# A fused attention, low-rank mixer and two MLPs on one core: new plan costs for the float32 products, earlier loads, other banks for the first scores, and products of ones in the plan's gaps

## The chip, the cores and the metric

The kernel runs on one core of a Trainium2 chip. The metric is the device time of one execution in microseconds (us); before the change it is 1762.4 us (median of 3 runs, 1760.25 to 1764.01). Engines are named as in the profile: PE (TensorE), DVE (VectorE), ACT (ScalarE), POOL (GpSimd) and SP (SyncE, which issues nearly all DMAs).

## The reference

An attention with mean-pooled keys and values, then a token mixer of rank 32 with an MLP, then a layer norm with a second MLP. Batch 8, 8 heads of 64, 576 positions, model width 512, MLP width 2048.

```
k_p, v_p = mean over groups of 8 positions of k, v          # 576 -> 72
scores   = q @ k_p.T / 8;  attn = exp(scores - max) / (sum + 1e-9)
x        = concat over heads of attn @ v_p                   # (8, 576, 512)

u = x + (x.T @ U @ V).T                                      # U 576x32, V 32x576
x = u + max(u @ w_ch1, 0) @ w_ch2                            # 512 -> 2048 -> 512

xn = (x - mean) / sqrt(var + 1e-6) * g_ln
out = x + max(xn @ w_ch1', 0) @ w_ch2'
```

U, V and the weights arrive as float64 words, which the kernel turns into float32 with five DVE or ACT operations on each tile of 512 words.

## The kernel before, in words

**The work.** A *pair* P is two heads of one batch; there are 32. Its steps on PE are five score products of 144 columns (`att_s`, L846), ten transposes of the exponentials (`att_t`, through `turn`, L399) and the products with the values. For the first eight pairs (`TM`) these are ten products of 65 columns (`tm_v`, L1028) and five products with U of 128 columns (`tm_g`, L1085), all in plain float32. Between them stand the row maximum (DVE, L871), the exponential (ACT, L880), copies out of PSUM (ACT or DVE, L404 and L406) and the division (DVE, L1049, L1056, L1066). The later pairs use float32r with the operand split into a high and a low part (L977, L978). The first MLP's first eight blocks of hidden channels run beside the attention, for groups of 512 tokens: `a_l1` (L1290, twelve products a block) and `a_l2` (L1318). The rest, three passes over nine groups of tokens, runs after it (L1519, L1607).

**The planner.** Each step is recorded by `Order.op` with the engines it may run on and what it costs there in ns. `schedule` plays all steps through on these costs and fixes the order of every engine's instructions. A step's priority is the PE time that was recorded before it (`clk`) plus a bias. The chip then runs each engine's list in that order, with semaphores where data or a buffer is awaited: a plan cost that is wrong changes an order, and no instruction's duration. The costs which the change touches are

```
att_s:  {PE: 4 * 2 * SP / 2.4}        # 240 ns a score product
tm_v:   {PE: 2 * len(tiles) * 200}    # 200 ns a product, 6 or 4 of them in a step
tm_g:   {PE: 5 * 240}                 # 240 ns a product, 5 in a step
cost *= SLOW if warm < 3000 else 1.0  # SLOW = 2.0: PE is planned at half rate until it was busy
```

**Buffers.** A buffer name is a ring of tiles: `q` 2, `k` 1, `v` 1, `xT` 5; the PSUM banks are `pa` 2 (sums of `a_l1`), `pbc` 2 (sums of `a_l2`) and `py` 4 (scores, transposes, value products). `att_load` issues k, q and v of a pair from SP; with one `k` tile the next pair's k waits until the last pair's was pooled (`att_prep`, L795, L798). `ones` is a constant 128x128 float32r tile that POOL fills at the start (L513).

Of the kernel before, what the change touches and what calls it, by code (L numbers as in the profile page):

```python
# [8 lines left out]
F32 = mybir.dt.float32  # L9
# [92 lines left out]

class Order:
    def __init__(self, nc, tc):
        self.nc, self.tc, self.ops, self.clk, self.bias = nc, tc, [], 0.0, 0.0

    def op(self, engs, fn, r=(), w=(), prio=None, size=0, full=False):
        o = Op()
        o.engs, o.fn, o.succs, o.size, o.full = engs, fn, [], size, full
        o.prio = (self.clk + self.bias) if prio is None else prio  # L110
        o.eng = o.end = o.start = None
        preds, bufs = set(), []
        for wr, lst in ((False, r), (True, w)):
            for x in lst:
                b, k = x if isinstance(x, tuple) else (x, None)
                if b not in bufs:
                    bufs.append(b)
                for k2, (lw, rd) in b.acc.items():
                    if k is None or k2 is None or k == k2:
                        if lw is not None:  # L120
                            preds.add(lw)
                        if wr:
                            preds.update(rd)
        for wr, lst in ((False, r), (True, w)):
            for x in lst:
                b, k = x if isinstance(x, tuple) else (x, None)
                if wr:
                    if k is None:
                        b.acc = {None: (o, [])}
                    else:  # L130
                        b.acc[k] = (o, [])
# [12 lines left out]
        o.ready = {e: 0.0 for e in engs}  # L144
        self.ops.append(o)
        if PE in engs:
            self.clk += engs[PE]
        return o


    def schedule(self):
# [6 lines left out]
        events, parked, order = [], {}, []  # L158
# [158 lines left out]
            at(e, free[e])  # L317
        self.total = max(o.end for o in self.ops)
        order.sort(key=lambda x: x[:2])
        return [o for _, _, o in order]  # L320

    def emit(self, pools, init):
        opened = set()
# [26 lines left out]
L_SAME = 100.0  # L350
L_PE = 320.0
L_ANY = 220.0
SLOW = 2.0
TURN = 98.0
CW = 2
KEEP = 50000.0
# [66 lines left out]
class Kern:  # L423
# [263 lines left out]
    def setup_v(self):  # L687
        nc, o = self.nc, self.o
        n = S // 4

        def load(raw):
            for c in range(4):
                o.op(
                    {SY: 450},
                    lambda e, c=c: e.dma_start(raw.t[c * RANK : (c + 1) * RANK, :n], self.V[:, c * n : c * n + n]),
                    w=[(raw, c)],
                    size=36864,
                )

        x = self.staged(n, load, "a")  # L700
        vh, vl = self.buf("vd"), self.buf("vd")
        o.op({ACT: c_act(n), DVE: c_fast(n)}, lambda e: copy(nc, e, vh.t, x.t[:, :n]), r=[x], w=[vh])
        o.op(
            {DVE: c_dve(n), GP: c_pool(n)},
            lambda e: e.tensor_sub(vl.t, x.t[:, :n], vh.t.bitcast(F32)),
            r=[x, vh],
            w=[vl],
        )
        for i, (y, copies) in enumerate(((vh, 3), (vl, 1))):
            d = Buf(None)  # L710
            for c in range(4):
                o.op(
                    {SY: 450},
                    lambda e, i=i, c=c, y=y: e.dma_start(
                        self.v_d[i, :, c * n : c * n + n], y.t[c * RANK : (c + 1) * RANK].bitcast(F32)
                    ),
                    r=[y],
                    w=[(d, c)],
                    size=18432,
                )  # L720
            for c in range(copies):
                r = (3 * i + c) * RANK
                o.op(
                    {SY: 450},
                    lambda e, i=i, r=r: e.dma_start(self.vst.t[r : r + RANK].bitcast(F32), self.v_d[i]),
                    r=[d],
                    w=[(self.vst, 3 * i + c)],
                    size=73728,
                )
# [43 lines left out]
    def att_load(self, P):  # L773
        o = self.o
        b, p = divmod(P, NP)
        q, k, v = self.buf("q"), self.buf("k"), self.buf("v")
        o.op({SY: 450}, lambda e: e.dma_start(k.t, self.kT[b, p]), w=[k], size=294912)
        o.op({SY: 450}, lambda e: e.dma_start(q.t, self.qT[b, p]), w=[q], size=294912)
        o.op(
            {SY: 450},  # L780
            lambda e: e.dma_start(v.t, self.v[b, 2 * p : 2 * p + 2].rearrange("h (k s) d -> k h (s d)", s=POOL)),
            w=[v],
            size=294912,
        )
        self.raw[P] = (q, k, v)

    def att_prep(self, P):
        nc, o = self.nc, self.o
        q, k, v = self.raw[P]
# [21 lines left out]

    def att_prep_v(self, P):
        o = self.o
        v = self.raw[P][2]
        vs = self.vs[P] = self.buf("v1" if P < TM else "vz" if P < LEAN_T else "vs")
        n = POOL * D
        while n > D:
            n //= 2
            to, w = (lambda n=n: v.t[:, :, :n]), [v]
# [4 lines left out]
            o.op(  # L824
                {GP: c_pool(2 * n), DVE: c_dve(2 * n)},
                lambda e, n=n, to=to: e.tensor_add(to(), v.t[:, :, :n], v.t[:, :, n : 2 * n]),
                w=w,
            )
        if P < LEAN_T:
# [1 line left out]
        self.split(  # L831
            View(vs, 0, lambda t: t[:, 0:4:3]),
            View(vs, 1, lambda t: t[:, 1:3]),
            View(v, None, lambda t: t[:, :, :D]),
            2 * D,
        )

    def att_s(self, P, t):
        q, kbd = self.qk[P]
        if t in (0, 3):  # L840
            self.sps[P, t // 3] = self.buf("py")
        ps = self.sps[P, t // 3]
        i = t % 3 * 2 * SP
        self.o.op(
            {PE: 4 * 2 * SP / 2.4},
            lambda e: e.matmul(  # L846
                ps.t[:, i : i + 2 * SP], q.t[:, QT[t] : QT[t] + 128], kbd.t.rearrange("p h n -> p (h n)"),
                start=True, stop=True, skip_group_check=True,
# [1 line left out]
            r=[q, kbd],  # L850
            w=[ps],
            full=True,
        )

    def att_m(self, P):
# [163 lines left out]
    def tm_v(self, P, z):  # L1019
# [11 lines left out]
                    )  # L1031

        r = [vs] + [(ef, j) for j in range(2 + z)]
        self.o.op({PE: 2 * len(tiles) * 200}, mm, r=r, w=[ps], full=True)

    def tm_n(self, P):
        o = self.o
# [36 lines left out]
    def tm_g(self, P):  # L1074
# [12 lines left out]
                )  # L1087

        r = [(x, (P, 0)), (x, (P, 1)), (x4, (P, 1)), self.us]
        self.o.op({PE: 5 * 240}, mm, r=r, w=[(pg, c)], full=True)  # L1090

    def tm_t(self, b, c):
        x, x4 = self.tx[b]
# [126 lines left out]
    def att_steps(self):  # L1220
# [6 lines left out]
        ld = lambda P: (lambda: self.att_load(P) if P < B * NP else None)  # L1227
        pr = lambda P: (lambda: self.att_prep(P))
        pv = lambda P: (lambda: self.att_prep_v(P))
        first = [ld(0), pr(0), pv(0), ld(1)] + [s(0, t) for t in range(5)] + [pr(1), pv(1), ld(2)]  # L1230
        first += [m(0)]
        for P in range(B * NP):
            N = P + 1
            last = P % NP == NP - 1
            S_ = [s(N, t) for t in range(5)] if N < B * NP else [None] * 5
            M_ = m(N) if N < B * NP else None
            R_ = [ld(P + 3), pr(P + 2), pv(P + 2)] if P + 2 < B * NP else [None] * 3
            T_ = [tt(P, j) for j in range(3)]
            V_ = [av(P, 0, 0), av(P, 1, 0), av(P, 0, 1), av(P, 1, 1)]
            if P < TM:  # L1240
                c = P % NP
                G = lambda c, P=P: [lambda: self.tm_g(P - P % NP + c)]
                W = [lambda P=P: self.tm_v(P, 0), lambda P=P: self.tm_v(P, 1), lambda P=P: self.tm_n(P)]
                seq = [S_[0], R_[2], S_[1], T_[0], S_[2], S_[3], T_[1], S_[4], T_[2], R_[1], M_]
# [6 lines left out]
                seq += [W[0], R_[0], W[1], W[2]]  # L1251
                if last:
                    b = P // NP
                    if b:
# [3 lines left out]
                    end = G(c) + [tt_[0], tt_[1], lambda b=b: self.att_gs(b), u[0], tt_[2], u[1], tt_[3], u[2], u[3], tt_[4], u[4]]  # L1258
                    seq += end
            elif not last:  # L1260
                seq = [S_[0], R_[2], S_[1], T_[0], S_[2], S_[3], T_[1], S_[4], T_[2], R_[1], M_, V_[0]]
                seq += [V_[1], R_[0], V_[2], V_[3]]
            else:
                b = P // NP
                x = [(lambda b=b, i=i: self.att_xt(b, i)) for i in range(5)]
                g = [(lambda b=b, i=i: self.att_g(b, i)) for i in range(5)]
                gs = lambda b=b: self.att_gs(b)
                vm = [(lambda b=b, h=h, c=c: self.att_vm(b, h, c)) for c in range(NCC) for h in range(2)]
                seq = [S_[0], R_[2], T_[0], S_[1], T_[1], S_[2], T_[2], V_[0], V_[1], S_[3], V_[2], V_[3], S_[4], R_[1]]
                seq += [M_, x[0], x[1], g[0], x[2], R_[0], g[1], x[3], g[2], x[4], g[3], g[4], gs]  # L1270
                seq += vm
            if P == 0:
                seq = first + seq
# [69 lines left out]
    def phase_a(self):  # L1343
# [2 lines left out]
        self.xT, self.xhl, self.ut, self.hid, self.wres = {}, {}, {}, {}, {}  # L1346
        self.ud, self.yd, self.wd = {}, {}, {}
        per = self.att_steps()
        self.lean = False
        for st in self.biased(per[0], E_BIAS):  # L1350
            st()
# [486 lines left out]
P_BIAS = -20000.0  # L1838
BACC = {"dynamic_dma_scratch_size": 2048}
TM = 2 * NP  # L1840
E_BIAS = -40000.0
LEAN_T = 8
LEAN_X = 8
W_LEAD = (-12000.0, 8000.0)
# [50 lines left out]
```

## Time and profile before

| | us |
|---|---|
| median of 3 runs | 1762.4 |
| the profiled execution | 1762.12 |
| its span, first to last instruction | 1760.3 |
| PE busy in the span | 1731.6 |
| PE busy in the first 140 us | 122.30 |
| DVE busy in the first 140 us | 117.32 |

The page gives the busy time of each engine; "idle before" in a row of the timeline is the time that the engine stood still ahead of that group of instructions and what ended it. In the trace a float32 product that isn't a transpose stands as two MATMUL records: the program's ten products of L1028 for a pair are a group of x20, its five score products x10. The granted clock is TensorE's, as a share of 2.4 GHz.

### The profile page before, as it was taken

What the parts mean: (1) busy time and instruction counts of PE and PEld (TensorE: products, weight loads), DVE (VectorE), ACT (ScalarE), POOL (GpSimd) and SP (SyncE); (2) the same over time, 40 slices, a digit from 0 to 9 for tenths busy, and PEclk for the clock granted to TensorE, in tenths of its full rate; (3) what the DMA queues carried; (4) which work ended last, traced back from release to release, by engine and by line L of the source; (5) the groups of instructions that cost most, each with busy time, mean ns of one, the idle gap of its engine ahead of it and who ended that gap; (6) DMA issues with size and microseconds to landing.
All of it is one profiled execution on the core that took longest, in us unless ns stands there. A gap on an engine that the chain in (4) does not pass through costs nothing.

```text
span 1760.3 us, 27152 instructions
## 1 busy us (share of the span) xinstructions
PE 1731.6 (98%) x10257; PEld 1526.3 (87%) x10257; DVE 975.9 (55%) x1834; ACT 732.0 (42%) x1843; POOL 790.9 (45%) x682
## 2 busy tenths in 40 slices
PE   7999999999999999999999999999999999999998
PEld 6788888888888889989999888999899999999897
DVE  6998887887745344444446866553224633333333
ACT  4665655655622224444444443333333432232221
POOL 3342222322100077777777863333335455555654
PEclk9999999999999999999999999999999999999999
DMA  6664654554243244444444344331112433333322
GB/s 191 197 193 161 208 173 139 192 182 131 98 147 121 79 166 120 121 120 120 120 120 113 128 129 154 131 128 66 48 49 85 144 102 102 105 120 105 102 78 78
DMA packets 96691, 222.99 MB, mean 127 GB/s; under 512 B 15408, under 2 KB 15792, under 8 KB 90800
## 3 DMA queue, kind: packets, MB, share of 16 engines
q1 hardware_dynamic: 96416, 221.26, 39.7%
q8 instruction: 80, 1.31, 0.3%
q14 instruction: 51, 0.42, 0.1%
q10 hardware_dynamic: 144, 0.00, 0.0%
HBM read 151.85 MB, written 69.37 MB: 126 GB/s over the span
## 4 chain that ended last, share of the span: by engine, by line
PE 87%; DVE 4%; DMA 2%; issue 0%; ACT 0%; DVEq 0%; SPq 0%; ACTq 0%
PE py L1607 33%; PE pa L1519 17%; PE pbc L1519 12%; PE pbc L1318 10%; PE pa L1290 9%; PE py L399 2%; PE py L846 1%; DMA wraw<-wC 1%; PE py L977 1%; PE py L978 1%; PE py L1184 0%; DMA w_d<-wx 0%; PE py L1015 0%; PE py L1014 0%; DMA xraw<-u_d 0%
## 5 line engine op out<-in xcount | busy, mean ns | idle before, releaser
L1607 PE MATMUL py<-hid,w2h 128*128 128x512 f32 x1728 | 541.3, 394 | 0.2 <-DVE hid L1547 0.2
L1607 PE MATMUL py<-hid,w2l 128*128 128x512 f32 x864 | 338.6, 392 | 0.0
L1519 PE MATMUL pa<-op,w1h 128*128 128x256 f32 x1728 | 326.1, 281 | 3.3 <-DVE pa L1583 3.0
L1519 PEld LDWEIGHTS pa<-op,w1h 128*128 128x128 f32 x1728 | 293.8, 188 | 40.2 <-DVE pa L1583 3.9
L1607 PEld LDWEIGHTS py<-hid,w2h 128*128 128x128 f32 x1728 | 273.6, 189 | 11.0 <-DVE hid L1547 0.5
L555 POOL TENSOR_TENSOR op<-xraw,op 128x512 fp32r<-128x512 f32 x130 | 171.3, 1321 | 247.5 <-ACT op L404 244.7
L1577 DVE TENSOR_TENSOR pbc<-s,pbc 128x512 f32<-128x512 f32 x108 | 75.1, 696 | 369.3 <-PE pbc L1519 369.1
L1519 PEld LDWEIGHTS pbc<-op,w1h 128*128 128x128 f32 x1296 | 220.6, 188 | 29.9 <-DVE s L406 1.8
L1519 PE MATMUL pbc<-op,w1h 128*128 128x256 f32 x1296 | 244.3, 281 | 1.4 <-DVE s L406 1.4
L1519 PE MATMUL pa<-op,w1l 128*128 128x256 f32 x864 | 242.6, 281 | 0.0
L1607 PEld LDWEIGHTS py<-hid,w2l 128*128 128x128 f32 x864 | 162.4, 188 | 36.7
L1318 PE MATMUL pbc<-op,wh 128*128 128x512 f32 x576 | 182.0, 397 | 0.0
L1519 PE MATMUL pbc<-op,w1l 128*128 128x256 f32 x648 | 181.8, 281 | 0.0
L1290 PE MATMUL pa<-hid,wh 128*128 128x512 f32 x576 | 180.4, 394 | 0.0
L1519 PEld LDWEIGHTS pa<-op,w1l 128*128 128x128 f32 x864 | 162.9, 189 | 0.0
L1547 DVE SCALAR_TENSOR_TENSOR hid<-pa,hid 128x512 fp32r<-128x512 f32 x108 | 74.5, 689 | 121.7 <-ACT hid L1541 121.6
L1541 ACT ACTIVATE hid<-pbc 128x512 fp32r<-128x512 f32 x108 | 64.7, 599 | 183.3 <-DVE pbc L1577 182.4
L1541 ACT ACTIVATE hid<-pa 128x512 fp32r<-128x512 f32 x108 | 64.6, 598 | 174.2 <-PE pa L1519 167.9
L1473 POOL TENSOR_TENSOR t<-xraw 128x512 f32<-128x512 f32 x52 | 67.8, 1305 | 131.8 <-DMA xraw<-n_d 73.0
L1290 PEld LDWEIGHTS pa<-hid,wh 128*128 128x128 f32 x576 | 105.8, 188 | 21.4 <-DVE op L1297 0.2
L1519 PEld LDWEIGHTS pbc<-op,w1l 128*128 128x128 f32 x648 | 121.9, 188 | 0.0
L1318 PEld LDWEIGHTS pbc<-op,wh 128*128 128x128 f32 x576 | 103.8, 188 | 19.4
(210 smaller groups left out, 2939.3 us busy)
## 6 DMA issues: line engine op xcount, KB each, us to landing
xraw<-n_d SPq DMA_DIRECT2D x18, 1024.0 KB
wraw<-wC SPq DMA_DIRECT2D x32, 512.0 KB
wraw<-wA SPq DMA_DIRECT2D x24, 512.0 KB
w_d<-wx SPq DMA_DIRECT2D x48, 256.0 KB
wraw<-w_d SPq DMA_DIRECT2D x48, 256.0 KB
k<-kT SPq DMA_DIRECT2D x32, 288.0 KB
q<-qT SPq DMA_DIRECT2D x32, 288.0 KB
v<-v SPq DMA_DIRECT2D x32, 288.0 KB
```

What stands on the lines that cost most here:

```text
L399: e.matmul(out, src, ident, start=first, stop=True, is_transpose=True, skip_group_check=True)
L555: lambda e: e.tensor_sub(lo(), src(), hi().bitcast(F32)),
L846: lambda e: e.matmul(ps.t[:, i : i + 2 * SP], q.t[:, QT[t] : QT[t] + 128], kbd.t.rearrange("p h n -> p (h n)"), start=True, stop=True, ski ...
L977: e.matmul(ps.t[:, :SH], w, eh.t[:, h, c], start=True, stop=False)
L1290: e.matmul(ps.t, w.t[:, c], u.t, start=(i == 0), stop=(i == 3 * NCC - 1))
L1318: e.matmul(ps.t, w.t[:, c], x.t, start=(f == 0 and j == 0), stop=(f == NA - 1 and j == 2))
L1473: o.op(on, lambda e: e.tensor_sub(dst(), a(), c()), r=r, w=w)
L1519: e.matmul(bank.t[:, sl], w.t[:, self.WCOL[k], c], u.t[:, t], start=(first and i == 0), stop=(last and i == 5), skip_group_check=True,)
L1541: lambda e: e.activation(h.t[:, :TG], bank.t, AF.Relu),
L1547: lambda e: e.scalar_tensor_tensor(l.t[:, :TG], bank.t, 0.0, h.t[:, :TG].bitcast(F32), op0=ALU.max, op1=ALU.subtract),
L1577: o.op({DVE: c_dve(TG)}, lambda e: e.tensor_add(c.t, s.t, c.t), r=[s], w=[c])
L1607: e.matmul(y.t, w.t[:, i, c], x.t[:, :TG], start=(first and q == 0), stop=(last and q == 2))
```

## The change

Seven edits, all of which act through the planner:

1. The PE costs of `att_s`, `tm_v` and `tm_g` become 123, 112 and 112 ns a product. Their old values stay as `lead`, what they add to the priorities' clock.
2. `SLOW` becomes 1.0: PE is planned at full rate throughout.
3. `filled` goes over the planned PE list. Where PE is planned idle between 1.3 and 140 us, it puts in as many products of `ones` with `ones` (512 columns, into a bank of `pa`, `pbc` or `py` that is planned free) as gaps of 225 ns fit. Their results are never read.
4. The k of pairs 1 and 3 goes to a tile of `xT` (`KX`), and v has a load step of its own (`att_load_v`), so that the first loads are issued as k, q, k, q, v.
5. Pooling of k of pair 1 is recorded ahead of v of pair 0.
6. The scores of the first four pairs (`EARLY`) go to `pa` instead of `py`.
7. `setup_v` loads V with one DMA instead of four, and writes each of its two parts with one instead of four.

```diff
-            self.clk += engs[PE]
+            self.clk += engs[PE] if lead is None else lead
...
+    def filled(self, order):
+        rings, fn = self.filler
...
+        extra, last = [], FILL[0]
+        for o in [o for o in order if o.eng == PE]:
+            if o.start > FILL[1]:
+                break
+            n = int((o.start - last) / FILL[2])
+            for k in range(n):
+                t = last + k * FILL[2]
+                best = None
+                for (r, i), spans in used.items():
+                    prev = max([e for s, e in spans if s <= t], default=-1e9)
+                    soon = min([s for s, e in spans if s > t], default=1e9)
+                    if prev + 500 <= t and soon >= o.start and (best is None or prev < best[0]):
+                        best = prev, r, i
+                if best is None:
+                    continue
+                z = Op()
+                z.eng, z.start, z.end, z.bufs = PE, t, t + FILL[2], ()
+                z.fn = lambda e, r=best[1], i=best[2]: fn(e, r.tiles[i])
+                extra.append(z)
+            last = o.end
...
-SLOW = 2.0
+SLOW = 1.0
...
-        q, k, v = self.buf("q"), self.buf("k"), self.buf("v")
+        q, k = self.buf("q"), self.buf("xT" if P in KX else "k")
...
-            self.sps[P, t // 3] = self.buf("py")
+            self.sps[P, t // 3] = self.buf("pa" if P < EARLY else "py")
...
-            {PE: 4 * 2 * SP / 2.4},
+            {PE: 123},
...
+            lead=4 * 2 * SP / 2.4,
...
-        self.o.op({PE: 2 * len(tiles) * 200}, mm, r=r, w=[ps], full=True)
+        self.o.op({PE: 2 * len(tiles) * 112}, mm, r=r, w=[ps], full=True, lead=2 * len(tiles) * 200)
...
-        self.o.op({PE: 5 * 240}, mm, r=r, w=[(pg, c)], full=True)
+        self.o.op({PE: 5 * 112}, mm, r=r, w=[(pg, c)], full=True, lead=5 * 240)
...
-        first = [ld(0), pr(0), pv(0), ld(1)] + [s(0, t) for t in range(5)] + [pr(1), pv(1), ld(2)]
+        first = [lk(0), lk(1), lv(0), pr(0), pr(1), lv(1), pv(0)] + [s(0, t) for t in range(5)] + [pv(1), lk(2), lv(2)]
...
+        self.o.filler = [self.R[a] for a in ("pa", "pbc", "py")], lambda e, ps: e.matmul(
+            ps, self.ones, self.ones.rearrange("p (o n) -> p o n", o=1).to_broadcast([128, 4, 128]),
+            start=True, stop=True, skip_group_check=True,
+        )
...
+KX = (1, 3)
...
+EARLY = 4
+FILL = (1300.0, 140000.0, 225.0)
```

All lines of the file move by about 40: L846, L1028, L1085, L399, L1290 and L1318 are L888, L1071, L1128, L439, L1334 and L1362 after it. The products of ones are L1393; the built program holds 155 of them, in 28 runs, and has the same other products on PE as before.

PE's list at the start of the program, from the scores of pair 0 to the value products of pair 0; before:

```order
L846 MATMUL py_253<-kbd_153,q_155 128x144 x3
L846 MATMUL py_254<-kbd_153,q_155 128x144 x2
L846 MATMUL py_255<-kbd_154,q_156 128x144 x2
L399 MATMUL py_256<-ident,sc_167 72x128 x4
L846 MATMUL py_255<-kbd_154,q_156 128x144
L846 MATMUL py_253<-kbd_154,q_156 128x144
L399 MATMUL py_254<-ident,sc_167 72x128 x4
L846 MATMUL py_253<-kbd_154,q_156 128x144
L399 MATMUL py_256<-ident,sc_167 72x64 x2
L1028 MATMUL py_254<-v_192,ef_166 128x65 x6
L1028 MATMUL py_256<-v_192,ef_166 128x65 x4
```

and now:

```order
L1393 MATMUL pa_249<-ones 128x512 x15
L888 MATMUL pa_249<-kbd_153,q_155 128x144 x3
L888 MATMUL pa_250<-kbd_153,q_155 128x144 x2
L1393 MATMUL pbc_251<-ones 128x512 x11
L888 MATMUL pa_249<-kbd_154,q_156 128x144 x3
L888 MATMUL pa_250<-kbd_154,q_156 128x144
L439 MATMUL py_253<-ident,sc_167 72x128 x4
L439 MATMUL py_254<-ident,sc_167 72x128 x4
L888 MATMUL pa_250<-kbd_154,q_156 128x144
L439 MATMUL py_255<-ident,sc_167 72x64 x2
L1393 MATMUL pbc_251<-ones 128x512 x3
L1071 MATMUL py_256<-v_192,ef_166 128x65 x6
```

29 products of ones stand among the first pair's work, 15 of them ahead of everything.

The same list at the value products of the pair of `vs_162` and the next scores, where the last of the products of ones stand; before, the MLP's products (L1318) stand there:

```order
L978 MATMUL py_253<-el_174,vs_162 128x288
L1318 MATMUL pbc_252<-op_200,wh_227 128x512
L1318 MATMUL pbc_252<-op_201,wh_227 128x512
L1318 MATMUL pbc_252<-op_200,wl_228 128x512
L1318 MATMUL pbc_252<-op_202,wh_229 128x512
L1318 MATMUL pbc_252<-op_203,wh_229 128x512
L1318 MATMUL pbc_252<-op_202,wl_230 128x512
L977 MATMUL py_255<-eh_173,vs_162 128x288
```

and now, down to the first product of the MLP behind them:

```order
L1021 MATMUL py_256<-el_174,vs_162 128x288
L1393 MATMUL pa_249<-ones 128x512 x4
L1020 MATMUL py_254<-eh_173,vs_162 128x288
L1021 MATMUL py_254<-el_174,vs_162 128x288
L1393 MATMUL pa_249<-ones 128x512 x7
L1020 MATMUL py_255<-eh_173,vs_162 128x288
L1021 MATMUL py_255<-el_174,vs_162 128x288
L1393 MATMUL pa_249<-ones 128x512 x12
L888 MATMUL py_253<-kbd_154,q_156 128x144 x3
L1393 MATMUL pa_249<-ones 128x512 x7
L1362 MATMUL pbc_251<-op_208,wh_235 128x512
```

The MLP's products have moved behind, and 30 products of ones stand in one pair's stretch.

SP's list of DMAs at the start, before:

```order
L777 DMA k0_157<-kT 128x576
L778 DMA q0_155<-qT 128x576
L781 DMA v0_158<-v 72x2x512
L778 DMA q1_156<-qT 128x576
L649 DMA wraw0_144<-U 128x4x32
L656 DMA wraw0_144<-U 64x32
L695 DMA araw0_150<-V 32x144 x4
L777 DMA k0_157<-kT 128x576
```

and now:

```order
L813 DMA k0_157<-kT 128x576
L814 DMA q0_155<-qT 128x576
L813 DMA xT0_177<-kT 128x576
L814 DMA q1_156<-qT 128x576
L823 DMA v0_158<-v 72x2x512
L689 DMA wraw0_144<-U 128x4x32
L696 DMA wraw0_144<-U 64x32
L813 DMA xT1_178<-kT 128x576
```

The k of pair 1 is the third DMA and no longer the eleventh; v of pair 0 stands two places later.

## Rows read from the trace of the kernel before

**Rows 1.** The page: the span; then busy time, its share and instructions.

```profile
span 1760.3 us, 27152 instructions
PE 1731.6 (98%) x10257; PEld 1526.3 (87%) x10257; DVE 975.9 (55%) x1834; ACT 732.0 (42%) x1843; POOL 790.9 (45%) x682
```

**Rows 2.** Busy time by stretch (stretch, length, engines, granted clock, DMA share, GB/s).

```profile
0.00:31.00 31.00, 20.05 (x84) 17.53 (x85) 18.73 (x55) 14.48 (x46) 7.95 (x26) 1.00 0.70 208
31.00:38.00 7.00, 5.74 (x43) 4.91 (x42) 4.99 (x12) 3.06 (x11) 3.93 (x6) 1.00 0.32 100
38.00:50.00 12.00, 11.27 (x55) 10.54 (x55) 8.46 (x20) 4.92 (x17) 3.98 (x5) 0.57 0.58 181
50.00:101.00 51.00, 46.31 (x319) 40.32 (x318) 49.53 (x112) 33.96 (x105) 21.92 (x20) 1.00 0.64 195
101.00:140.00 39.00, 38.93 (x214) 32.55 (x212) 35.61 (x71) 25.72 (x82) 14.78 (x14) 1.00 0.63 207
sum 140.00, PE 122.30 PEld 105.86 DVE 117.32 ACT 82.13 POOL 52.56; mean PE 24.46 PEld 21.17 DVE 23.46 ACT 16.43 POOL 10.51
```

**Rows 3.** Timeline of PE, 5 to 34 us (start, us, ..., idle before and its end).

```profile
5.10 2.74 PE L846 MATMUL py<-kbd,q 128*128 128x144 f32 x10 [5.10 <-DVE kbd L413]
12.48 1.30 PE L846 MATMUL py<-kbd,q 128*128 128x144 f32 x4 [4.65 <-DVE kbd L413]
...
17.71 4.50 PE L1028 MATMUL py<-v,ef 72*128 72x65 f32 x20 [0.42 <-ACT ef L404]
22.00 1.27 PE L846 MATMUL py<-kbd,q 128*128 128x144 f32 x4
23.06 1.06 PE L399 MATMUL py<-ident,sc 128*72 128x128 f32 x4
23.92 0.69 PE L846 MATMUL py<-kbd,q 128*128 128x144 f32 x2
```

**Rows 4.** Timeline of PE, 49 to 54 us.

```profile
49.99 1.16 PE L1085 MATMUL pbc<-xg,us 128*128 128x128 f32 x8
50.99 0.39 PE L1085 MATMUL pbc<-x,us 128*128 128x128 f32 x2
51.21 2.34 PE L1028 MATMUL py<-v,ef 72*128 72x65 f32 x20
53.39 0.71 PE L846 MATMUL py<-kbd,q 128*128 128x144 f32 x4
53.94 0.60 PE L399 MATMUL py<-ident,sc 128*72 128x128 f32 x4
54.37 0.41 PE L846 MATMUL py<-kbd,q 128*128 128x144 f32 x2
```

**Rows 5.** Timeline of PE, 104 to 105 us.

```profile
104.13 0.62 PE L1290 MATMUL pa<-hid,wh 128*128 128x512 f32 x2
104.59 0.39 PE L1290 MATMUL pa<-hid,wl 128*128 128x512 f32 x1
104.82 0.62 PE L1290 MATMUL pa<-hid,wh 128*128 128x512 f32 x2
```

**Rows 6.** Timeline of POOL: the fill of the constant tile.

```profile
1.25 0.21 POOL L513 MEMSET ones<- 128x128 f32 x1
```

**Rows 7.** Timeline of PE at a change from float32 to float32r, 184 us.

```profile
184.13 0.30 PE L399 MATMUL py<-ident,sc 64*72 64x64 f32 x2
184.37 0.74 PE L1318 MATMUL pbc<-op,wh 128*128 128x512 f32 x2
184.95 0.40 PE L1318 MATMUL pbc<-op,wl 128*128 128x512 f32 x1
185.18 0.63 PE L1318 MATMUL pbc<-op,wh 128*128 128x512 f32 x2
```

More of the change, by code (lines that the diff above doesn't have):

```diff
@@ L104, in __init__, with op @@
     def __init__(self, nc, tc):
-        self.nc, self.tc, self.ops, self.clk, self.bias = nc, tc, [], 0.0, 0.0
-    def op(self, engs, fn, r=(), w=(), prio=None, size=0, full=False):
+        self.nc, self.tc, self.ops, self.clk, self.bias, self.filler = nc, tc, [], 0.0, 0.0, None
+    def op(self, engs, fn, r=(), w=(), prio=None, size=0, full=False, lead=None):
         o = Op()
@@ L319, in schedule @@
         order.sort(key=lambda x: x[:2])
-        return [o for _, _, o in order]
+        return self.filled([o for _, _, o in order])
+    def filled(self, order):
+        rings, fn = self.filler
+        used = {(r, i): [] for r in rings for i in range(r.n)}
+        life = {}
+        for o in order:
+            for b in o.bufs:
+                if b.ring in rings:
+                    x = life.setdefault(b, [o.start, o.end])
+                    x[1] = max(x[1], o.end)
+        for b, span in life.items():
+            used[b.ring, b.slot].append(span)
+        extra, last = [], FILL[0]
[18 more added lines that the diff above has]
+            last = o.end
+        out, k = [], 0
+        for o in order:
+            while k < len(extra) and extra[k].start < o.start:
+                out.append(extra[k])
+                k += 1
+            out.append(o)
+        return out
     def emit(self, pools, init):
@@ L691, in load @@
         def load(raw):
[L692 to L698, printed above, removed]
+            o.op(
+                {SY: 450},
+                lambda e: e.dma_start(raw.t[:, :n], self.V.rearrange("r (c n) -> c r n", n=n)),
+                w=[raw],
+                size=147456,
+            )
         x = self.staged(n, load, "a")
@@ L710, in setup_v @@
             d = Buf(None)
[L711 to L720, printed above, removed]
+            o.op(
+                {SY: 450},
+                lambda e, i=i, y=y: e.dma_start(self.v_d[i].rearrange("r (c n) -> c r n", n=n), y.t.bitcast(F32)),
+                r=[y],
+                w=[d],
+                size=73728,
+            )
             for c in range(copies):
@@ L775, in att_load, with att_load_v @@
         b, p = divmod(P, NP)
-        q, k, v = self.buf("q"), self.buf("k"), self.buf("v")
+        q, k = self.buf("q"), self.buf("xT" if P in KX else "k")
         o.op({SY: 450}, lambda e: e.dma_start(k.t, self.kT[b, p]), w=[k], size=294912)
         o.op({SY: 450}, lambda e: e.dma_start(q.t, self.qT[b, p]), w=[q], size=294912)
-        o.op(
+        self.raw[P] = (q, k)
+    def att_load_v(self, P):
+        b, p = divmod(P, NP)
+        v = self.buf(VX.get(P, "v"))
+        to = (lambda: v.t.bitcast(F32)[:, :, : POOL * D]) if P in VX else (lambda: v.t)
+        self.o.op(
             {SY: 450},
-            lambda e: e.dma_start(v.t, self.v[b, 2 * p : 2 * p + 2].rearrange("h (k s) d -> k h (s d)", s=POOL)),
+            lambda e: e.dma_start(to(), self.v[b, 2 * p : 2 * p + 2].rearrange("h (k s) d -> k h (s d)", s=POOL)),
             w=[v],
@@ L784, in att_load @@
         )
-        self.raw[P] = (q, k, v)
+        self.raw[P] += ((v, to),)
     def att_prep(self, P):
         nc, o = self.nc, self.o
-        q, k, v = self.raw[P]
+        q, k = self.raw[P][:2]
         kp, kbd = self.buf("kp"), self.buf("kbd")
@@ L813, in att_prep_v @@
         o = self.o
-        v = self.raw[P][2]
+        v, vt = self.raw[P][2]
         vs = self.vs[P] = self.buf("v1" if P < TM else "vz" if P < LEAN_T else "vs")
@@ L818, in att_prep_v @@
             n //= 2
-            to, w = (lambda n=n: v.t[:, :, :n]), [v]
+            to, w = (lambda n=n: vt()[:, :, :n]), [v]
             if P < LEAN_T and n == D:
@@ L825, in att_prep_v @@
                 {GP: c_pool(2 * n), DVE: c_dve(2 * n)},
-                lambda e, n=n, to=to: e.tensor_add(to(), v.t[:, :, :n], v.t[:, :, n : 2 * n]),
+                lambda e, n=n, to=to: e.tensor_add(to(), vt()[:, :, :n], vt()[:, :, n : 2 * n]),
                 w=w,
@@ L833, in att_prep_v @@
             View(vs, 1, lambda t: t[:, 1:3]),
-            View(v, None, lambda t: t[:, :, :D]),
+            View(v, None, lambda t: vt()[:, :, :D]),
             2 * D,
@@ L1226, in att_steps @@
         av = lambda P, h, f: (lambda: self.att_av(P, h, f))
-        ld = lambda P: (lambda: self.att_load(P) if P < B * NP else None)
+        lk = lambda P: (lambda: self.att_load(P) if P < B * NP else None)
+        lv = lambda P: (lambda: self.att_load_v(P) if P < B * NP else None)
         pr = lambda P: (lambda: self.att_prep(P))
         pv = lambda P: (lambda: self.att_prep_v(P))
-        first = [ld(0), pr(0), pv(0), ld(1)] + [s(0, t) for t in range(5)] + [pr(1), pv(1), ld(2)]
+        first = [lk(0), lk(1), lv(0), pr(0), pr(1), lv(1), pv(0)] + [s(0, t) for t in range(5)] + [pv(1), lk(2), lv(2)]
         first += [m(0)]
@@ L1236, in att_steps @@
             M_ = m(N) if N < B * NP else None
-            R_ = [ld(P + 3), pr(P + 2), pv(P + 2)] if P + 2 < B * NP else [None] * 3
+            R_ = [lk(P + 3), lv(P + 3), pr(P + 2), pv(P + 2)] if P + 2 < B * NP else [None] * 4
             T_ = [tt(P, j) for j in range(3)]
@@ L1243, in att_steps @@
                 W = [lambda P=P: self.tm_v(P, 0), lambda P=P: self.tm_v(P, 1), lambda P=P: self.tm_n(P)]
[L1244 removed]
+                seq = [S_[0], R_[3], S_[1], T_[0], S_[2], S_[3], T_[1], S_[4], T_[2], R_[2], M_]
                 if c and P < NP:
@@ L1250, in att_steps @@
                     seq += [self.setup_v]
-                seq += [W[0], R_[0], W[1], W[2]]
+                seq += [W[0], R_[0], R_[1], W[1], W[2]]
                 if last:
@@ L1260, in att_steps @@
             elif not last:
-                seq = [S_[0], R_[2], S_[1], T_[0], S_[2], S_[3], T_[1], S_[4], T_[2], R_[1], M_, V_[0]]
-                seq += [V_[1], R_[0], V_[2], V_[3]]
+                seq = [S_[0], R_[3], S_[1], T_[0], S_[2], S_[3], T_[1], S_[4], T_[2], R_[2], M_, V_[0]]
+                seq += [V_[1], R_[0], R_[1], V_[2], V_[3]]
             else:
@@ L1268, in att_steps @@
                 vm = [(lambda b=b, h=h, c=c: self.att_vm(b, h, c)) for c in range(NCC) for h in range(2)]
-                seq = [S_[0], R_[2], T_[0], S_[1], T_[1], S_[2], T_[2], V_[0], V_[1], S_[3], V_[2], V_[3], S_[4], R_[1]]
-                seq += [M_, x[0], x[1], g[0], x[2], R_[0], g[1], x[3], g[2], x[4], g[3], g[4], gs]
+                seq = [S_[0], R_[3], T_[0], S_[1], T_[1], S_[2], T_[2], V_[0], V_[1], S_[3], V_[2], V_[3], S_[4], R_[2]]
+                seq += [M_, x[0], x[1], g[0], x[2], R_[0], R_[1], g[1], x[3], g[2], x[4], g[3], g[4], gs]
                 seq += vm
@@ L1348, in phase_a @@
         per = self.att_steps()
+        self.o.filler = [self.R[a] for a in ("pa", "pbc", "py")], lambda e, ps: e.matmul(
+            ps, self.ones, self.ones.rearrange("p (o n) -> p o n", o=1).to_broadcast([128, 4, 128]),
+            start=True, stop=True, skip_group_check=True,
+        )
         self.lean = False
@@ L1840 @@
 TM = 2 * NP
+KX = (1, 3)
+VX = {}
 E_BIAS = -40000.0
+EARLY = 4
+FILL = (1300.0, 140000.0, 225.0)
 LEAN_T = 8
```

## The prediction

> **What bounds the kernel.** I read the page's busy times first: PE is busy 1731.6 of 1760.3 us [rows 1], so the time is PE's own work, what it loses at a low clock, and some 29 us of standing still. The table by stretches then shows where: in the first 140 us PE is busy 122.30, so 17.7 us of the 28.7 idle ones lie there [rows 1, 2]. The change adds nothing behind that point, so the case is decided in the head.
>
> The timeline of PE shows the second loss in the head. Four records of the scores take 1.06 us from start to next start at 22.00, and 0.55 at 53.39; the twenty records of the value products 4.29 us at 17.71, and 2.18 at 51.21; four transposes 0.86 at 23.06 against 0.43 at 53.94 [rows 3, 4]. PE thus runs at the lower of its two levels (1.2 of 2.4 GHz) from 5 to about 31 us, and again from 38 to 50, where the granted clock is 0.57 [rows 2]. The column prints 1.00 for the first 31 us, but the durations there are the low level's, and I go by them. The ratio is 1.93 to 1.97; I take 1.97 of the longest group.
>
> **The change part by part.**
>
> *What it gives back: low clock.* PE is busy 20.05 us up to 31 and 11.27 from 38 to 50 [rows 2], together 31.3. At the full clock it would be 31.3 / 1.97 = 15.9, so 15.4 us can come back. With products of ones in nearly all gaps PE hardly stands still, and from 50 to 101 us the granted clock is 1.00 although PE is idle for 4.7 us of that stretch [rows 2]. I take all of it, but the first products of ones run at the low level themselves: 0.229 (below) times 0.97 = 0.22 us more for each. Between none and all of the first 15 (3.3 us) I take nine, 2.0 us. Net -13.4.
>
> *What it gives back: idle time.* The 17.7 us of the head are 5.10 ahead of the first scores, 4.65 ahead of the second pair's [rows 3], and 8 us of small waits. The second pair's k is now the third DMA and needs no free `k` tile, so the wait of 4.65 should go whatever stands in it; the rest is filled by products of ones. What stays: PE can't start one until `ones` is there at 1.46 (1.25 + 0.21) [rows 6], 1.5 us; and waits that a product of ones doesn't cover, since the plan's gaps lie elsewhere than the chip's. Their bounds are 0 and all idle time but the first wait, 17.7 - 5.1 = 12.6. I take 3, nearer to the low end, since the list is now so full that PE comes late to most things. Net -17.7 + 4.5 = -13.2.
>
> *What it adds.* 155 products of ones. The trace has no such row; the nearest is the MLP's product of 512 columns in float32r with a weight load each, three of which take 0.69 us (104.13 to 104.82), 0.229 each [rows 5]. 155 x 0.229 = 35.5 us. PE takes its list in order, so one that stands where nothing was idle costs its whole 0.229 us, and one in a real gap nothing; in this sum they count in full and the idle time that they fill is taken off above. For the price of one the bounds are the shortest product of the trace, 0.108 for 128 columns (four transposes from 53.94 to 54.37) [rows 4], and 0.45 (this row at the low level, which the term above has); I take 0.229, the row with the same columns and type.
>
> Twenty-eight runs of float32r products among float32 ones add up to 15 changes of kind. Behind a transpose the first three MLP products take 0.81 us (184.37 to 185.18) instead of 0.69, 0.12 more [rows 7]: +1.7, with 0 as the other end.
>
> *Why the plan has so many.* 155 x 0.225 is 35 us of planned gaps, more than the 17.7 that PE really stands idle in the head. The new costs explain it. A float32 product stands as two records, so that the cost of one record is half a product: ten value products are twenty records and take 2.18 us, five with U 1.22 (49.99 to 51.21), two scores 0.55 [rows 4]. The plan now has 10 x 0.112 = 1.12, 5 x 0.112 = 0.56 and 0.123 each. For each of the first eight pairs it thinks PE free for 1.06 + 0.66 + 5 x 0.152 = 2.5 us in which PE in truth still multiplies: 20 us, some 87 products of ones, in gaps that the chip doesn't have. The same holds for the end of the head, where 30 of them stand in one pair's stretch, in the place of MLP products which PE had to do without any wait (PE is busy 38.93 of 39 us from 101 to 140 [rows 2]) and now does later.
>
> *What costs nothing by itself.* The other banks for four pairs' scores, the separate v loads and the single DMAs for V only move waits inside the head, and the idle term holds them. V of pair 0 is loaded two places later; its sums are needed only by the value products at 17.71, so there is cover. A product of ones adds a wait: it needs its bank's last reader done, planned 0.5 us earlier, and all of PE's list is queued behind it, the next pair's scores first, whose maximum DVE waits for. I count that in the 3 us. DVE must do its 117.3 us of the first 140 as well [rows 2]; if PE comes to the end of the head some 10 us later than now, DVE has those as slack, so PE stays the bound.
>
> *The sum.* -13.4 - 13.2 + 35.5 + 1.7 = +10.6 us. On the profiled execution's 1762.1 that is 1772.7, and since that one lies 0.3 under the median of the runs, 1773.
>
> The nearest row isn't the only price on offer. The Trainium skill, "TensorE: Matmul & The Clock Gate", section "Back-to-back issue gap", gives about 131 ns for a product of 512 columns in a sustained stream, and about 216 ns for one by itself. The trace disagrees with the first: 229 ns in the densest stretch [rows 5]. By the second the sum would be 2.0 us less; by the first 15.2 less, 1758, which would turn the sign.
>
> **The rivals.**
>
> *A: as above*, 1773. Its own range follows from the bounds: without any residual wait, change of kind or low-clock product 1766, with half of the 12.6 us 1776.
>
> *B: the waits stay.* PE is late, but DVE is nearly full: 49.53 of 51 us from 50 to 101 [rows 2]. If DVE's list, which is made for a PE twice as fast in float32, has PE wait at other places than the filled ones, the residual is the full 12.6 instead of 3: 1773 + 9.6 = 1783. For it: DVE has little room after 50 us. Against it: 18 us of DVE's first 50 are idle, and PE comes later.
>
> *C: the products of ones vanish in time that was lost anyway, and the kernel is faster.* Lost now are 17.7 + 15.4 = 33.1 us, and 35.5 are put in. If a product of ones cost less than a product of the MLP, as all of a run have the same weights and the same columns, the sign turns at (33.1 - 4.5 - 2.0 - 1.7) / 155 = 0.161 us each. At the far bound of 0.108 the term is 16.7 instead of 35.5, and the time 1773 - 18.8 = 1754. Against it: the MLP's rows go at 0.229 without a break although their weight loads lie beside them, so that the columns set the pace and not the weights. The lower of the page's two figures would speak for it.
>
> *D: no change that can be seen.* Rival A's low end, and the 11.0 us of idle time behind 140 us (28.7 - 17.7) [rows 1, 2], which another order may shorten by some us: 1764.
>
> *E: the clock doesn't rise.* If products of ones keep it at the low level in the first 50 us, the 68 ahead of the last scores of the sixth pair at 0.22 us more each, cost 15.0 us in place of 2.0, and the 15.4 don't come back: 1773 + 13.0 + 15.4 = 1801. Against it: the clock rises in the kernel before with much less on PE.
>
> **How the numbers follow.** A measurement of this kernel tells about 0.2% from no change, 3.5 us: faster is under 1758.9, slower over 1765.9. A has 0.67, B 0.14, D 0.10, C 0.07, E 0.02. A, B and E are slower but for 0.01 of A (0.82); that 0.01, D and the 0.01 of C next to the turn of the sign are no change (0.12), and the rest of C is faster (0.06). The predicted time is A's, 1773. The range leaves out C, E and the ends of B and D: 1764 to 1785.
>
> **What would show it.** In the new profile the rows of L1393 should start about 1.5 us and come to 155, at 0.23 us from start to start once the clock is up. The value products of the head (L1071) should take 2.2 us for twenty records from the second pair on, and the granted clock of 38 to 50 us be 1.00. PE's idle time up to 140 us should be near 5 us instead of 17.7, and the first MLP product (L1334, now L1290) come a few us earlier than now, but the MLP products behind the last run of ones 5 to 12 us later than the same products now. It is wrong in its size if PE stands idle more than 10 us in the head, and in its sign if a product of ones takes under 0.16 us or if much of the idle time behind 140 us goes.

## The result

The changed kernel takes 1771.16 us (median of 6 runs, 1770.14 to 1774.35) against 1762.1 us for the kernel before (6 runs, 1759.83 to 1764.01): ratio 1.0051, 95% interval 1.0037 to 1.0066. It is slower by 9 us; forecast were 1773 us and +10.6.

The profiled execution took 1774.35 us, the longest of the six. Its busy time by stretch, in the columns of [rows 2] and to be read against its rows:

```profile
0.00:31.00 31.00, 29.49 (x182) 25.98 (x183) 17.70 (x60) 17.17 (x59) 8.27 (x28) 1.00 0.68 191
31.00:38.00 7.00, 7.00 (x52) 6.34 (x51) 2.85 (x11) 2.24 (x9) 2.56 (x2) 1.00 0.70 204
38.00:50.00 12.00, 12.00 (x86) 10.49 (x85) 8.03 (x24) 7.42 (x26) 3.70 (x6) 1.00 0.58 170
50.00:101.00 51.00, 51.00 (x324) 44.49 (x323) 39.86 (x97) 27.71 (x82) 21.37 (x24) 1.00 0.58 174
101.00:140.00 39.00, 38.40 (x207) 31.40 (x207) 35.99 (x72) 29.55 (x100) 13.59 (x12) 1.00 0.63 189
```

PE is idle for 2.1 us of the first 140 where it was idle for 17.7, the clock of 38 to 50 us is 1.00 where it was 0.57, and DVE is busy 39.86 of 51 us where it was 49.53: PE is now the full engine, with products of ones. Its timeline at the start and at two later places (as in [rows 3, 4]):

```profile
1.51 6.15 PE L1393 MATMUL pa<-ones 128*128 128x512 f32 x15 [1.51 <-POOL ones L553]
7.50 1.39 PE L888 MATMUL pa<-kbd,q 128*128 128x144 f32 x10
8.63 2.80 PE L1393 MATMUL pbc<-ones 128*128 128x512 f32 x11
11.26 1.14 PE L888 MATMUL pa<-kbd,q 128*128 128x144 f32 x8
...
14.49 2.34 PE L1071 MATMUL py<-v,ef 72*128 72x65 f32 x20
16.64 1.18 PE L1393 MATMUL pbc<-ones 128*128 128x512 f32 x4
...
58.06 0.71 PE L1334 MATMUL pa<-hid,wh 128*128 128x512 f32 x2
...
126.24 2.91 PE L1393 MATMUL pa<-ones 128*128 128x512 f32 x12
129.75 0.97 PE L888 MATMUL py<-kbd,q 128*128 128x144 f32 x6 [0.60 <-ACT wh L444]
130.47 1.88 PE L1393 MATMUL pa<-ones 128*128 128x512 f32 x7
```

The first 15 products take 5.99 us, 0.40 each, so most of them run at 1.2 GHz (the clock's column prints 1.00 there, as it did before). From 7.50 us on all work is at the full clock: the twenty records of the value products take 2.15 us at 14.49 where they took 4.29 at 17.71. The first MLP product comes at 58.06, 10.6 us earlier than before (68.63), and the one behind the last run of ones at 132.18, 10.7 us later than the same product before (121.50).

All executions share a mark behind the head: the first product of the layer norm with `ones`. This is the view of its line, before and after (durations min/median/max, then first and last start):

```profile
L1726 PE MATMUL pbc<-lnh,ones x9: 393/394/394, 665.5 to 1012.2; 128*128 128x512 f32 x9
```

```profile
L1774 PE MATMUL pbc<-lnh,ones x9: 393/394/394, 669.9 to 1016.6; 128*128 128x512 f32 x9
```

The head has lost 4.4 us between these two executions. The spans differ by 12.3, so 7.9 more lie behind the mark. Part of them are waits of PE, here first before, then in the changed kernel:

```profile
PE pa L1519 <- DVE pa L1583: 3.0, 2, 2.0
```

```profile
PE pa L1567 <- DVE pa L1631: 7.4, 3, 4.6
PE pa L1393 <- POOL ones L553: 1.5, 1, 1.5
PE pbc L1567 <- DVE s L446: 1.4, 1, 1.4
PE py L888 <- ACT wh L444: 0.6, 1, 0.6
```

L1631 is the line that was L1583, and the wait for it has grown by 4.4 us. Its longest part ends at 1075 us. First DVE's timeline there, then PE's stretches (PE, PEld, DVE, ACT, POOL, clock):

```profile
1071.01 0.43 DVE L635 TENSOR_SCALAR wt<-wraw 128x512 int32<-128x512 int32 x1 [9.06 <-DMA wraw<-wC]
...
1074.53 0.42 DVE L1631 TENSOR_TENSOR pa<-s,pa 128x256 f32<-128x256 f32 x1
```

```profile
1070.00:1075.00 5.00, 0.37 (x2) 0.00 (x0) 3.80 (x8) 1.15 (x4) 0.00 (x0) 1.00 0.06 12
1075.00:1080.00 5.00, 5.00 (x23) 4.58 (x24) 2.14 (x4) 1.54 (x3) 0.29 (x1) 0.66 0.47 152
```

DVE stands for 9.06 us before a decode step whose weights come late; the addition that PE wants is behind it in DVE's list, PE stops for 4.63 us, and the clock is 0.66 in the 5 us behind it. It is also 0.76 and 0.90 in the two stretches of 5 us from 1035 on, where it was 1.00 before. Experiment e7 asks whether that belongs to the change.

### The profile page after: what moved, and what is told of

Read it like the earlier page. It is cut to its first block, busy times and chain, and to the rows that moved or that the text cites. A ratio compares the mean times of both kernels' runs of the same rounds, so it can differ in the third digit from the quotient of the medians.

```text
span 1772.6 us, 27429 instructions
## 1 busy us (share of the span) xinstructions
PE 1755.4 (99%) x10412; PEld 1546.4 (87%) x10412; DVE 973.7 (55%) x1843; ACT 733.6 (41%) x1849; POOL 777.2 (44%) x667
## 4 chain that ended last, share of the span: by engine, by line
PE 94%; DVE 3%; DMA 1%; issue 1%; POOL 1%; ACT 0%; DVEq 0%; ACTq 0%; POOLq 0%
PE py L1655 32%; PE pa L1567 17%; PE pbc L1567 12%; PE pbc L1362 11%; PE pa L1334 11%; PE py L439 3%; PE py L888 2%; PE pbc L1393 1%; DMA wraw<-wC 1%; PE py L1071 1%; PE py L1020 1%; PE py L1021 1%; PE pa L1393 1%; PE py L1058 0%; PE py L1057 0%
## 5 line engine op out<-in xcount | busy, mean ns | idle before, releaser
L595 POOL TENSOR_TENSOR op<-xraw,op 128x512 fp32r<-128x512 f32 x130 | 171.2, 1320 | 252.1 <-ACT op L444 248.0
L1362 PE MATMUL pbc<-op,wh 128*128 128x512 f32 x576 | 181.4, 396 | 0.0
L1334 PE MATMUL pa<-hid,wh 128*128 128x512 f32 x576 | 180.3, 394 | 0.1
L1334 PEld LDWEIGHTS pa<-hid,wh 128*128 128x128 f32 x576 | 105.9, 188 | 21.5 <-DVE op L1341 0.3
L1362 PEld LDWEIGHTS pbc<-op,wh 128*128 128x128 f32 x576 | 104.3, 188 | 19.4
```

The lines of the kernel that those rows point to most:

```text
L595: lambda e: e.tensor_sub(lo(), src(), hi().bitcast(F32)),
L1334: e.matmul(ps.t, w.t[:, c], u.t, start=(i == 0), stop=(i == 3 * NCC - 1))
L1362: e.matmul(ps.t, w.t[:, c], x.t, start=(f == 0 and j == 0), stop=(f == NA - 1 and j == 2))
```

## The experiments

Ratios are to the kernel before, timed beside each set on the same chip. "Mark" is the first norm product in the profiled execution; idle time is PE's in the first 140 us.

| | ones | ratio, 95% interval | mark, us | idle, us |
|---|---|---|---|---|
| before | 0 | 1 | 665.5 | 17.7 |
| changed | 155 | 1.0051, 1.0037 to 1.0066 | 669.9 | 2.1 |
| e1 changed, no ones | 0 | 1.0048, 1.0031 to 1.0065 | 669.0 | 24.9 |
| e2 changed, each twice | 310 | 1.0235, 1.0215 to 1.0255 | 703.0 | 1.5 |
| e12 changed, every second | 78 | 1.0019, 1.0008 to 1.0029 | 663.8 | 9.0 |
| e3 old costs | 81 | 1.0011, 1.0000 to 1.0022 | 663.3 | 7.7 |
| e4 old costs, no ones | 0 | 1.0022, 1.0009 to 1.0036 | 666.0 | 17.9 |
| e9 old costs, ones up to 50 us | 45 | 1.0019, 1.0008 to 1.0031 | 664.3 | 10.9 |
| e6 old costs, loads and banks | 93 | 1.0020, 1.0009 to 1.0030 | 665.1 | 6.2 |
| e5 new costs alone | 0 | 1.0028, 1.0018 to 1.0038 | 664.0 | 20.3 |
| e10 full rate alone | 0 | 1.0007, 0.9997 to 1.0017 | 662.8 | 18.9 |
| e11 loads and banks alone | 0 | 1.0005, 0.9993 to 1.0017 | 664.6 | 18.5 |
| e7 changed, later decode | 155 | 1.0049, 1.0036 to 1.0062 | 670.0 | 2.1 |
| e8 before, later decode | 0 | 1.0003, 0.9990 to 1.0015 | 668.2 | 19.1 |

The kernel before, and those without products of ones, scatter: 26 runs of the one before in one set lie between 1753.8 and 1764.6 us with mean granted clocks of 0.992 to 0.999, and the four of e2 between 1800.8 and 1802.1 with 0.999 and 1.000. A mark is one execution's, so differences of 2 or 3 us between marks of kernels without ones say nothing; the ratios do. "Up to the mark" below means sums over PE's records from the start to that product: the time from each record's start to the next, without PE's idle time.

**e1: no products of ones.**

```diff
-FILL = (1300.0, 140000.0, 225.0)
+FILL = (1300.0, 1300.0, 225.0)
```

Expected: 

> The changed kernel without its 155 products of ones, every other instruction in the same order. Theory (most of the products stand where PE isn't idle and cost their full 0.23 to 0.25 us): their 40 us go, some idle time and some low clock come back, 1751 to 1766 us, at the least 5 us under the changed kernel's 1771. Rival (they stand in time that is lost anyway, and the loss lies in the new order): 1771 or, with the clock low again in the head, up to 1780.

1767.65 us, between the two ranges; the ratio is that of the changed kernel within its interval. The theory failed: 155 products of ones went, and the mark moved by 0.9 us. The stretches show what took the time:

```profile
0.00:31.00 31.00, 21.61 (x153) 19.85 (x154) 18.80 (x61) 17.43 (x59) 9.07 (x29) 1.00 0.71 199
31.00:50.00 19.00, 16.34 (x116) 14.47 (x116) 13.14 (x36) 12.21 (x37) 7.13 (x10) 0.91 0.59 182
50.00:101.00 51.00, 45.83 (x273) 39.50 (x273) 39.74 (x96) 26.08 (x78) 19.94 (x22) 0.94 0.55 172
101.00:140.00 39.00, 31.34 (x157) 25.11 (x156) 35.07 (x71) 29.26 (x103) 13.66 (x12) 0.86 0.59 190
```

PE is idle for 24.9 us instead of 2.1, and the clock is down in every stretch from 31 us on. Up to the mark the products of ones gave up 40.5 us; idle time takes back 22.9, and the same other records, at the lower clock, are 16.8 us longer.

**e2: each twice.**

```diff
-                extra.append(z)
+                extra += [z, z]
```

Expected: 

> Each of the 155 products of ones issued twice. Theory (PE has no idle time left in the head, and one costs what an MLP product of 512 columns costs): +155 x 0.229 = +35.5 us, 1806. Rival (one costs under 0.16 us, since weights and columns repeat, or still finds idle time): under 1796.

1801.32 us. The mark moved by 33.1 us for 155 more products, 0.2135 us each. So PE has no free time left among them, and rival C's price of 0.161 is excluded. A product by itself takes more than 0.2135, as its own rows in this trace show, with products of the MLP ahead of them:

```profile
112.14 0.62 PE L1334 MATMUL pa<-hid,wh 128*128 128x512 f32 x2
112.61 0.40 PE L1334 MATMUL pa<-hid,wl 128*128 128x512 f32 x1
112.84 0.62 PE L1334 MATMUL pa<-hid,wh 128*128 128x512 f32 x2
113.30 0.40 PE L1334 MATMUL pa<-hid,wl 128*128 128x512 f32 x1
113.53 6.55 PE L1393 MATMUL pbc<-ones 128*128 128x512 f32 x28
119.93 0.60 PE L439 MATMUL py<-ident,xg 128*128 128x128 f32 x4
```

28 products of ones take 6.40 us, 0.229 each, and the six MLP products ahead of them 1.39 us, 0.232 each: the price in the sum was right. The mark moved by less because PE's idle time and the other records up to the mark fell by 0.7 us each, and three fewer of the first products ran at the low clock.

**e12: every second one.**

```diff
+        extra = extra[::2]
         out, k = [], 0
```

Expected: 

> The changed kernel with every second product of ones left out, 78 of 155 remaining in their places. Theory (155 fill PE beyond all idle time; fewer still hold the clock, and then DVE sets the end of the head): the first product of the norm at 663 to 667 us against 669.9, PE idle 8 to 16 us in the first 140 and the clock near 1.00, the time 0.2 to 0.4% over the kernel before against 0.5. Rival (as with none and with all: what a product takes, idle time and a lower clock take back): 669 to 670 us and 0.45 to 0.55%.

1762.92 us, mark 663.8: as the theory had it, with a ratio just under its range:

```profile
0.00:31.00 31.00, 27.94 (x183) 24.53 (x184) 18.85 (x61) 17.46 (x59) 9.52 (x29) 1.00 0.69 202
31.00:50.00 19.00, 18.69 (x140) 16.31 (x140) 13.31 (x38) 12.63 (x38) 6.89 (x9) 1.00 0.65 208
50.00:101.00 51.00, 48.96 (x298) 41.02 (x296) 42.67 (x98) 28.26 (x84) 21.60 (x23) 1.00 0.55 168
101.00:140.00 39.00, 35.45 (x189) 28.56 (x189) 35.02 (x73) 30.94 (x110) 16.82 (x15) 0.96 0.61 198
```

78 products hold the clock nearly as well as 155, and PE's idle time is 9.0 us and not 24.9. With none, 78, 155 and 310 in the same order of work the ratio is 1.0048, 1.0019, 1.0051, 1.0235: too few cost the clock and idle time, too many cost themselves. Of the change's 0.51%, 0.32 goes with the other 77 products.

**e3 and e4: the old plan costs, with the products that they call for and without.**

```diff
-            {PE: 123},
+            {PE: 4 * 2 * SP / 2.4},
...
-        self.o.op({PE: 2 * len(tiles) * 112}, mm,
+        self.o.op({PE: 2 * len(tiles) * 200}, mm,
...
-        self.o.op({PE: 5 * 112}, mm,
+        self.o.op({PE: 5 * 240}, mm,
```

Expected of e3: 

> The changed kernel with the plan's old costs of the float32 products (240, 200 and 240 ns a product), so that 81 products of ones remain. Theory (the halved costs made gaps which the chip doesn't have): 74 products less, 17 us, less up to 5 us of idle time that comes back: 1754 to 1759, under the kernel before. Rival (the costs don't matter, the loss comes from the other order or a late load behind the head): 1768 to 1773.

Expected of e4: 

> As the one with the old costs, and no products of ones. Theory (in true gaps a product of ones is nearly free and holds the clock up): 3 to 12 us slower than with the 81, near 1762. Rival (products of ones never pay): as fast as with the 81 or faster, under 1757.

e3 takes 1762.64 us, 0.40% less than the changed kernel, with an interval that reaches down to 1: the direction of the theory, but not under the kernel before. The intervals of e3, with the old costs and 81 products, and of e12, with the halved costs and 78, overlap. e4 takes 1764.08 us, 0.11% over e3, less than expected, and the intervals overlap. Without any products the halved costs are the slower list, 1.0048 (e1) against 1.0022 (e4): the list counts as well as the number of products, and with some 80 of them the two lists can't be told apart.

**e5, e10, e11, e6: the other edits by themselves.** e5 is the kernel before with the three costs and `lead`; e10 has `SLOW = 1.0` alone; e11 has the loads and banks alone (e4 with `SLOW = 2.0`); e6 is e3 with

```diff
-KX = (1, 3)
+KX = ()
-EARLY = 4
+EARLY = 0
```

and the old list `first`; the single DMAs for V stay.

Expected of e5: 

> The kernel before with nothing but the new plan costs of the float32 products (and the old ones as lead). Theory (the halved costs make an order in which PE waits more): the first product of the norm, at 665.5 us before, 2 to 4 us later, and the time 0.2 to 0.4% over the kernel before. Rival (the costs harm only by the products of ones that they call for): within 0.1%.

Expected of e10: 

> The kernel before with nothing but the plan at full rate (SLOW 1.0). Theory (a plan that takes PE for fast, with the clock low on the chip, has PE's list in a worse order, as the halved costs do): 0.1 to 0.2% over the kernel before. Rival (it is the loads or the banks that cost, as the kernel with old costs and no products is 0.22% over): within 0.1%.

Expected of e11: 

> Old plan costs, no products of ones, half rate at the start of the plan as before; the early loads, the single DMAs and the scores in pa remain. Theory: within 0.1% of the kernel before, the second pair's wait of 4.65 us gone and given back at other places. Rival (the loads or banks are what costs 0.22% in the kernel with old costs and no products): 0.15 to 0.3% over.

Expected of e6: 

> Products of ones (93 of them) and the plan at full rate, with the old costs, the old first loads and the scores of all pairs in py. Theory (in a plan with true costs the products pay for themselves, and the loads and banks bring nothing): the first product of the norm at 662 to 665 us, the time 0 to 0.2% under the kernel before. Rival (the early loads make the gain that the products alone don't have): first product of the norm at 666 or later.

The halved costs alone make the kernel 0.28% slower, as the theory had it, though the profiled mark (664.0, at the low end of that kernel's runs) doesn't show it. Full rate alone is undecided (0.07%, interval over 1), and so are loads and banks (0.05%): they bring nothing that can be measured. The wait of 4.65 us for the second pair's k [rows 3] is gone in e11, and PE's idle time in the head is 18.5 us all the same. e6, with its mark at the edge of the expected range, is 0.20% slower and not faster: a miss.

**e9: products of ones only up to 50 us of the plan.**

```diff
-FILL = (1300.0, 140000.0, 225.0)
+FILL = (1300.0, 50000.0, 225.0)
```

Expected: 

> Old plan costs, and products of ones only up to 50 us of the plan, 45 of them. Theory (a product pays where it holds the clock up, and is a loss of 0.21 us each where PE has other work or the clock holds without it): 36 products less than with all 81, up to 7 us; first product of the norm at 657 to 662 us, the time 0.1 to 0.3% under the kernel before. Rival (the late ones hold the clock and fill idle time too): as with 81, 0.1% over the kernel before.

1763.18 us, a miss. From 101 to 140 us PE is busy 31.38 of 39 us at a clock of 0.84, where e3 has 34.62 at 0.96. PE had come to that stretch early and waits there (4.6 us of it for DVE's L595); the kernel before, which came late, is busy there for 38.93 of 39 us [rows 2]. The rows of e9 and of e3:

```profile
101.00:140.00 39.00, 31.38 (x142) 24.33 (x142) 35.41 (x72) 29.13 (x105) 17.89 (x21) 0.84 0.54 158
```

```profile
101.00:140.00 39.00, 34.62 (x178) 27.45 (x177) 36.18 (x74) 29.76 (x110) 19.02 (x22) 0.96 0.53 161
```

**e7 and e8: the decode of the second MLP's weights two units later.**

```diff
-            bg.setdefault(nu + 6 + i * (nu - 12) // len(h), []).append(lambda f=f, z=z: self.ahead(1, f, z))
+            bg.setdefault(nu + 8 + i * (nu - 14) // len(h), []).append(lambda f=f, z=z: self.ahead(1, f, z))
```

Expected of e7: 

> The changed kernel with the background decode of the second MLP's weights started two units later, so that its loads don't meet the burst at 1040 to 1060 us. Theory (4 to 5 of the 9 us that the change costs are the wait of PE behind DVE's wait for a load of wC at 1062 to 1071 us): the wait for DVE L1631 falls from 7.4 to under 4 us, the time 4 to 6 us under the changed kernel's, 0.15 to 0.3% over the kernel before; the first product of the norm stays at 669.9. Rival (that wait is the profiled execution's alone, or turns up at another place): within 2 us of the changed kernel, 0.4 to 0.6% over the one before.

Expected of e8: 

> The kernel before with the same later start of the background decode. Theory (it has the same wait, smaller): waits for DVE L1583 fall from 3.0 to 1 us or less, the time 1 to 3 us lower. Rival: no difference.

The wait is no longer 4.6 us long in e7,

```profile
PE pa L1567 <- DVE pa L1631: 3.8, 2, 2.9
```

and the span behind the mark is 1766.0 - 670.0 = 1096.0 us, as in all other profiled executions (1094.8 to 1097.3) except the changed kernel's own, 1102.7. But the ratio stays at 1.0049, and with 4 us less it would be under that interval. The kernels with the old decode have no long wait either: in every profiled execution but the changed kernel's the longest one for this line is 1.7 to 2.9 us. So the 7.9 us behind the mark belong to that execution and not to the change, and the rival is right. e8 shows no difference.

## Why the prediction was right

The time and the sign held, 1771.2 for 1773, and so did the account of the change as products of ones that take more than they give back. In two things it was less right than the number: its gains and costs add up to another size in the traces, so that the near hit is in part luck, and the reason that it gave for the loss holds by half. Its terms, by what the runs showed:

- **Idle time**, -13.2 forecast: -15.6 in the first 140 us, -16.1 up to the mark. What stays is 1.51 at the start, as forecast, and 0.60 instead of 3.
- **Low clock**, -15.4 forecast: -20.0, by the time that all records but those of ones take up to the mark: 7.0 less for the scores (320 records, 0.141 us each before and 0.119 now), 4.5 for the transposes, 4.1 for the value products, 2.7 for those with U and 1.7 for the rest. It comes back in full, and the float32 products get shorter than the rows at the full clock said, since they now stand in longer runs: five scores take 1.13 us (7.50 to 8.63), 0.226 each, where two took 0.55 [rows 4]. The recorded ratio of 1.93 to 1.97 leaves out its own transposes, which give 2.00.
- **What is added**, +35.5, +2.0 and +1.7, together 39.2 forecast: 40.5 from the starts of all 28 runs to the next rows' starts, less idle time. The parts were nearly right as well: 35.4 for 155 at the 0.2286 of e2's row of 28, 2.6 for the low clock of the first 15 (5.99 us less 15 x 0.2286), and 2.5 left for changes between float32 and float32r and the like. Of the 28 runs 19 begin behind a float32 product (transposes included), and the first of each takes 0.31 to 0.34 us, some 0.10 more than in the middle of a run.
- **The sum** of these is +4.4 up to the mark, as the marks differ, where +10.6 was forecast: both gains were set too small. The medians differ by 9, and no trace shows where the rest lies. The changed kernel's profiled execution was 3.2 us over its median, the one before (1762.12) at the median of the six runs beside it, but over the medians of all later sets (1759.2 to 1760.3). With the usual 1096 us behind the mark and 2 us around the span, the median of 1759.2 in e7's set puts the usual mark of the kernel before near 661.5, and e7's own is 670.0. That is worked out, not seen in a trace; if it holds, the usual execution before loses less in the head than the profiled one, from whose rows the forecast took both gains.
- **Why so many**: the text held that some 87 of the 155 stand in gaps that the chip doesn't have, and so that the loss is theirs. e1 contradicts it as it stands: without any, PE is idle for 24.9 us and the kernel is as slow. e12 and e3 bear out the half of it that matters: about 77 can go, and 6 us with them. The step failed in leaving out what the missing products do to the clock and to idle time, and what the halved costs do to the order by themselves: 0.28% (e5), with no product of ones.
- **Behind the head** nothing was forecast, and the ratio of e7 bears it out, though the profiled execution seemed to deny it.
- **Rival C** is excluded by the price, 0.229 us with the same weights and columns in each, as much as an MLP product. **Rival B** is what the kernels with fewer products run into: from 101 to 140 us PE waits for DVE in e3, e4 and e9. **E** is excluded by the value products at 14.49. **D** is excluded by the interval.

No kernel of this study is faster than the kernel before. Whether 20 to 60 products, thinly spread up to 140 us in a plan with true costs, would be, wasn't tried.

## What to carry to other kernels

Products that only keep TensorE busy have an optimum in number: here, in one order of work, 78 beat none and 155, doubling showed the price of each, and even 78 did not beat the kernel before. Before a measured duration goes into a planner, count how many records one instruction leaves in the trace: a cost that is half the truth gave a slower order by itself here (0.28%, e5), and it makes gaps in the plan that the chip doesn't have. And an early stage that is made faster gives the time back where the next engine (here DVE, from 101 us on) isn't ready: look at what the late start had been hiding.

## What the runs showed of the hardware that was not expected

- A product of 512 columns with `ones` on both sides takes 0.229 us in a full list (28 in 6.40 us, e2), as an MLP product of the same size does [rows 5]: repeated weights and a result that nobody reads make it no cheaper. The Trainium skill, "TensorE: Matmul & The Clock Gate", section "Back-to-back issue gap", gives 216 ns for one by itself, 6% less; no run here shows its 131 ns of a sustained stream.
- The first product of ones behind a float32 product takes 0.31 to 0.34 us from its start to the next one's (19 runs of the changed kernel), behind a float32r product 0.22 to 0.24 (8 runs).
- The kernel before scatters over 10.8 us between executions on one chip (1753.8 to 1764.6), with mean clocks from 0.992 to 0.999; the four runs of e2, whose clock is 0.999 or 1.000, over 1.3.
- A load of 512 KB issued at 1056.32 us let DVE go on at 1071.01, 14.7 us later.
